# Chunk-selected attention with a squared-ReLU feed-forward: the last sequence's scores on row halves, its mask spread by DMA

## The chip, the cores and the metric

The kernel runs on one core of a Trainium2 chip. Its time is device microseconds of one execution; several executions are given by their median and range. The engines are called PE (TensorE, matrix products; PEld is its weight loads), DVE (VectorE), ACT (ScalarE), POOL (GpSimd) and SP (SyncE, which here only issues DMAs). Each works through its own instructions in order, and so does each queue of DMAs.

## The reference, cut to what matters

Four sequences of 768 positions, eight heads of 64. Keys are cut into 24 chunks of 32. For each query and head an upper bound of its product with any key of a chunk is formed from the chunk's elementwise minimum and maximum; the six chunks with the largest bound (among those not in the future) are kept, and plain causal softmax attention runs over the kept chunks. All of it then goes through a feed-forward layer with a squared ReLU.

```
k_min, k_max = min and max of k over each chunk
ub = sum(maximum(q * k_min, q * k_max), axis=-1)       # one number per query and chunk
ub = where(causal, ub, -1e9)
top_chunks = argsort(ub)[..., -6:]
scores = q @ k.T / sqrt(64)
scores = where(chosen chunk and not in the future, scores, -1e9)
attn = softmax(scores) @ v
x = attn as [3072, 512]
out = maximum(x @ w_in, 0) ** 2 @ w_out                # w_in 512x2048, w_out 2048x512
```

## The kernel before, in words

**Tiles.** A sequence has six tiles of 128 positions. The first tile can choose among at most four chunks, so it needs no selection; the first tiles of all four sequences are treated together at the start (`first_transposes`, `first_attention`, L553 to L605), with their own feed-forward. The other five tiles of each sequence follow, by pairs of heads: sixteen pairs, p = 0 to 15, four for each sequence.

**Stage A of a pair** (`stage_a`, L622) prepares keys and queries with the head dimension on partitions (for sequences 0 and 1 PE turns them, for 2 and 3 the DMA does, `turn_by_dma`, L388), takes chunk minima and maxima on DVE (L697), forms the bounds on PE (L660, L662), finds the sixth largest by MAX8 on DVE (L668) and writes the selection `selb` (L727: 1 where a chunk is not chosen). The selection is turned (by PE, or for sequences 2 and 3 by an SP DMA transpose) and copied under the 64 rows of the queries, into rows 64 to 87 of `qsc`; rows 64 to 87 of `kqc` hold -32768 in the columns of the respective chunk (`kq_rows`, L336). A product over 88 rows is then the score, pushed far down where the chunk isn't chosen. Each pair needs two key copies, two query copies and four selection copies for this, on DVE or ACT (helper `copy`, L281 and L283). Four sets of `kqc` and `qsc` rotate.

**Stage B of a pair** (`stage_b`, L766) has, for each head, five banks of 512 score columns (table `BANKS`): two matmuls of 88 rows (L782), the exponential on ACT (L804), a causal product on DVE or select on POOL for the 128x128 diagonal blocks (`causal`, L756), and four value matmuls with 65 columns (L793; the 65th is the sum of the weights). DVE divides (`normalise`, L609) and writes `x`.

**Feed-forward** (`ffn`, L823): `x` is turned (by DMA for sequences 1 to 3), `up` multiplies by w_in (L866), takes the ReLU (ACT L873, or DVE L875) and the square on DVE (L884), `down` multiplies by w_out (L897), copies the result out of PSUM and stores it with an SP DMA (L910). For the last sequence, `up` uses the score banks.

**What sets the order.** Every operation is given to a planner (class `Plan`, L81) with its engine or engines, a cost, a due time, what it needs and the buffers that it uses. The planner walks through a modelled time: among the operations that could start first on an engine it takes the one due first, and it writes out each engine's list. Buffers of a kind are counted in `Plan({...})` (L266). The due times come from numbers in `P` (L240): a lead for each pair's stage A, a due time and rate for each feed-forward, and so on. Early in the kernel, where the modelled PE waits, it puts in filler products of a constant tile (`keep_warm`, L529) to keep PE active. Loads go through POOL's queue in a fixed order.

The feed-forward work of a sequence is laid among the attention work of the next one; that of the last sequence has nothing beside it.

## Time and profile before

| what | us |
|---|---|
| median of 3 runs | 265.79 |
| lowest, highest | 264.72, 266.02 |
| span of the profiled execution, first to last instruction | 263.6 |
| PE busy in it | 251.4 |
| ACT busy in it | 197.8 |
| DVE busy in it | 183.0 |
| POOL busy in it | 106.4 |

The profiled execution has its span alone as a time of its own; it lies 2.2 us below the median of the runs, which also hold what comes before the first and after the last instruction. In the views below, a row of a group ends with its busy time, the mean of one instruction in nanoseconds, and the time that the engine sat idle just before such an instruction, with what ended that wait. Rows of the chain and of the timeline begin with start and duration in us. Matmuls overlap in their latency: what a stream of them costs is read from the distance of their starts.

### The profile page before, as it was taken

The numbers are of one execution on the slowest core, as the hardware profiler recorded it, in microseconds if no ns is written. First come the engines' busy times: TensorE is split into PE (matmuls) and PEld (weight loads), VectorE is DVE, ScalarE is ACT, GpSimd is POOL, SyncE is SP. The second block draws the span as 40 slices with busy tenths as digits, with TensorE's granted clock in tenths as the row PEclk, the third lists the DMA queues.
The fourth block names the chain that finished last, engine by engine and source line by source line (L and its number), as shares of the span: only waits on it lengthen the run. The fifth ranks groups of instructions, "written<-read, shape, count | busy, mean of one in ns | idle before, by whom it ended". The sixth has DMA issues, their size and how long they took to land.

```text
span 263.6 us, 6555 instructions
## 1 busy us (share of the span) xinstructions
PE 251.4 (95%) x2382; PEld 164.1 (62%) x2405; DVE 183.0 (69%) x663; ACT 197.8 (75%) x395; POOL 106.4 (40%) x185
## 2 busy tenths in 40 slices
PE   6899999999999999999999999998999999999995
PEld 1577566666687666665686645666865564765443
DVE  7569999778999999998999943644757142455000
ACT  6658897859899999999989845987866692677111
POOL 7998987799555599833311201110200010000000
PEclk9799999999999999999999999999999999999999
DMA  8999999999999999995440001154000113400122
GB/s 153 156 175 180 181 198 190 94 126 174 170 151 166 149 157 143 123 145 148 87 93 15 2 20 75 44 82 101 2 0 15 42 44 99 120 2 0 40 82 80
DMA packets 106336, 26.51 MB, mean 101 GB/s; under 512 B 99008, under 2 KB 103360, under 8 KB 106304
## 3 DMA queue, kind: packets, MB, share of 16 engines
q0 software_dynamic: 75088, 13.11, 67.9%
q1 hardware_dynamic: 31216, 12.98, 24.0%
q8 instruction: 19, 0.31, 0.5%
q14 instruction: 13, 0.11, 0.2%
HBM read 27.26 MB, written 6.29 MB: 127 GB/s over the span
## 4 chain that ended last, share of the span: by engine, by line
PE 62%; DVE 24%; ACT 8%; issue 3%; DMA 2%; SPq 0%; ACTq 0%; DVEq 0%
PE py L897 25%; PE ph L866 20%; PE ps L782 8%; PE av L793 4%; DVE h L884 4%; DVE kr L697 4%; DVE m L668 3%; DVE qsc L283 3%; ACT e L804 2%; DMA xT<-x 2%; ACT ht L873 2%; DVE x L614 2%; ACT qsc L281 2%; DVE kqc L283 1%; DVE ubm L722 1%
## 5 line engine op out<-in xcount | busy, mean ns | idle before, releaser
L866 PE MATMUL ph<-xT,w_in_sb 128*128 128x256 bf16 (+2 forms) x592 | 95.7, 304 | 1.6 <-DMA xT<-x 1.2
L804 ACT ACTIVATE e<-ps 128x512 bf16<-128x512 f32 x160 | 86.4, 608 | 7.5 <-PE ps L782 4.4
L897 PE MATMUL py<-w_out_sb,h 128*128 128x512 bf16 (+2 forms) x377 | 87.9, 370 | 1.2
L762 POOL TENSOR_SCALAR_AFFINE_SELECT e<-e 128x128 bf16<-128x128 bf16 (+1 forms) x88 | 31.0, 365 | 101.0 <-ACT e L804 89.1
L866 PEld LDWEIGHTS <-w_in_sb 128*128 128x128 bf16 x592 | 55.6, 97 | 24.9 <-DMA xT<-x 1.6
L873 ACT ACTIVATE ht<-ph 128x384 bf16<-128x384 f32 (+2 forms) x130 | 58.9, 457 | 16.2 <-PE ph L866 12.5
L884 DVE TENSOR_TENSOR h<-ht 128x256 bf16<-128x256 bf16 (+2 forms) x148 | 47.8, 333 | 16.4 <-ACT ht L873 12.9
L897 PEld LDWEIGHTS <-h 128*128 128x128 bf16 x400 | 36.2, 97 | 33.8
L782 PE MATMUL ps<-qsc,kqc 88*128 88x128 bf16 (+1 forms) x320 | 51.7, 272 | 0.3 <-DVE ubm L722 0.2
L782 PEld LDWEIGHTS <-kqc 88*128 88x128 bf16 x320 | 27.6, 97 | 14.8 <-issue 0.8
L281 ACT COPY ob<-py 128x512 f32<-128x512 f32 (+2 forms) x22 | 12.5, 570 | 29.2 <-PE py L897 29.1
L793 PEld LDWEIGHTS <-e 128*128 128x128 bf16 x640 | 29.6, 97 | 6.4 <-issue 0.3
L793 PE MATMUL av<-vn,e 128*128 128x65 bf16 x480 | 29.6, 193 | 0.0
L759 DVE TENSOR_TENSOR e<-e,tri 128x128 bf16<-128x128 bf16 (+1 forms) x40 | 9.7, 242 | 14.9 <-ACT e L804 14.2
L614 DVE TENSOR_TENSOR x<-av,rc 128x320 bf16<-128x320 f32 (+1 forms) x40 | 18.7, 472 | 0.5
L668 DVE MAX8 m<-ubm 128x8 f32<-128x24 f32 x160 | 15.5, 167 | 0.0
L697 DVE TENSOR_REDUCE kr<-kT 128x24 bf16<-128x768 bf16 x16 | 14.8, 951 | 0.2
L697 DVE TENSOR_REDUCE kr<-kt 128x24 bf16<-128x768 bf16 x16 | 14.8, 935 | 0.0
L793 PE MATMUL av<-v,e 128*128 128x65 bf16 x160 | 13.9, 193 | 0.1
L875 DVE TENSOR_SCALAR ht<-ph 128x256 bf16<-128x256 f32 (+2 forms) x18 | 8.2, 454 | 8.2 <-PE ph L866 8.2
L612 DVE RECIPROCAL rc<-av 128x5 f32<-128x5 f32 (+1 forms) x40 | 7.2, 184 | 9.4 <-PE av L793 8.5
L281 ACT COPY qsc<-sT 24x256 bf16<-24x256 bf16 (+1 forms) x29 | 12.4, 427 | 1.6 <-DMA sT<-selb 0.9
(92 smaller groups left out, 258.7 us busy)
## 6 DMA issues: line engine op xcount, KB each, us to landing
out_dram<-ob SPq DMA_DIRECT2D x23, 256.0 KB, 2.2
w_in_sb<-in_moe_w_in_dram POOLq DMA_DIRECT2D x4, 512.0 KB, 7.2
w_out_sb<-in_moe_w_out_dram POOLq DMA_DIRECT2D x4, 512.0 KB, 8.8
vn<-in_v_dram POOLq DMA_DIRECT2D x15, 128.0 KB, 6.9
nt<-in_k_dram POOLq DMA_DIRECT2D x10, 128.0 KB, 6.6
nt<-in_q_dram POOLq DMA_DIRECT2D x10, 128.0 KB, 5.3
kn<-in_k_dram POOLq DMA_DIRECT2D x8, 80.0 KB, 7.0
qn<-in_q_dram POOLq DMA_DIRECT2D x8, 80.0 KB, 5.7
```

Source lines behind the costliest of these rows:

```text
L281: nc.scalar.copy(dst, src)
L614: return plan.op({"DVE": 0.06 + 0.00108 * D * n}, due, lambda _: nc.vector.tensor_mul(x(), av[:, :, 0:D], rc[:, 0:n].unsqueeze(2).to_broad ...
L668: nc.vector.max(out=m8[:, i, hh], in_=ubm[:, i, hh])
L697: nc.vector.tensor_reduce(kr[:, mm].rearrange("d (t c) -> d t c", c=128 // CH) if b >= BY_DMA else kr[:, mm], part(kT).rearrange("d t (c j ...
L762: nc.gpsimd.affine_select(out=e, in_=e, compare_op=ALU.is_ge, fill=0.0, base=0, channel_multiplier=-1, pattern=[[0, n], [1, 128]])
L782: nc.tensor.matmul(ps[:, 128 * c:128 * (c + nt)], lhsT=kqs[:, s, hh, 128 * j:128 * (j + 1)], rhs=qss[:, s, hh, 128 * (t0 - 1):128 * (t0 - ...
L793: nc.tensor.matmul(av[:, t - 1], lhsT=e[:, 128 * c:128 * (c + 1)], rhs=value_tile(b, h, j), start=(i == 0 and c == 0), stop=(i == len(BANK ...
L804: nc.scalar.activation(e.tile, ps.tile, ACT.Exp, scale=scale), [sc], [ps, e])
L866: nc.tensor.matmul(ph.tile, lhsT=w_in_sb[:, ki, 128 * f:128 * (f + 1)], rhs=xT[:, c0 // 128:c1 // 128, ki], start=(ki == 0), stop=(ki == N ...
L873: nc.scalar.activation(ht.tile, ph.tile, ACT.Relu)
L884: {"DVE": 0.067 + w / 1920}, at[0] + P["h2"], lambda _: nc.vector.tensor_mul(h2[f][:, c0:c1], ht.tile, ht.tile), [op], [ht, h2[f]])))
L897: nc.tensor.matmul(py.tile, lhsT=h2[f][:, 128 * t:128 * (t + 1)], rhs=w_out_sb[:, f, c0:c1], start=(f == 0), stop=(f == NFI - 1))
```

## The change

For the last sequence alone (`MASKED = 3`), scores and mask part ways:

- The scores are products over the 64 rows of the head dimension, straight from the turned keys and queries. A pair's two heads lie on partitions 0 to 63 and 64 to 127, and `score_banks` issues them alternately, 128 columns each, so that one head uses one half of PE's rows and the other head the other. Two banks of each head are one operation of 16 matmuls; there are ten such operations.
- The selection (now 1 where a chunk is chosen) is multiplied by 3e38, turned by the SP DMA as before, stored to a DRAM buffer `seen`, and read back by four SP DMAs, each of which repeats every chunk's row over 32 partitions. What lands in `mask` (128 x 21 x 2 x 128) has 3e38 where the key's chunk is chosen by the query, and 0 elsewhere. POOL makes it causal at the five diagonal places.
- After the exponential, DVE takes the minimum of weights and mask (`choose`), for whole banks.
- The extra rows and the copies of keys, queries and selections are no longer made for this sequence.

To make room, two buffers that hold `kqc` and `qsc` for two sets each, the keys and queries of sequence 1 and the masks share three slots (`set`); `kq` falls from 6 to 4 buffers, `e` rises from 6 to 8. The ten output stores of sequences 1 and 2 go from SP's queue to POOL's (`out=(1, 2)`). The planner knows a cost of 0.095 for a switch between 64-row and full matmuls, and its layout is refitted: 249 shifts of due times over ranges of operations (`moves`), a new order of the loads (`order`), another tie width (`wait`).

The diff, cut to its core (the tables of shifts, renamed helpers and moved code left out):

```diff
     BUSY = 0.11
     WARM = 8.0
+    SWITCH = 0.095
...
+                if op.rows != rows:
+                    cost += self.SWITCH
+                rows = op.rows
...
-    P = dict(lead=[0, 207.45, 109.14, 153.29, -29.2, 112.12, 38.49, 53.35, 112.23, 30.95,
+    P = dict(moves=[], order=[], out=(1, 2), lead=[0, 207.45, 109.14, 153.29, -29.2, 112.12, 38.49, 53.35, 112.23, 30.95,
...
+    P.update(moves=[(702, 770, 14.04), (644, 759, -9.08), (940, 964, 20.66), (410,
+             423, 4.85), (679, 756, -9.73), (498, 570, 5.54), (535, 639, 3.35),
...
+             order=[0, 5, 3, 1, 2, 4, 6, 7, 10, 9, 19, 12, 11, 8, 13, 14, 15, 16,
...
+             wait=0.00328)
...
-    plan = Plan({"tp": 1, "ps": 3, "av": 2, "ff": 2, "e": 6, "h2": NFI + 6, "ht": 3,
-                 "ob": 3, "kq": 6, "nt": 6,
+    plan = Plan({"tp": 1, "ps": 3, "av": 2, "ff": 2, "e": 8, "h2": NFI + 6, "ht": 3,
+                 "ob": 3, "kq": 4, "nt": 6, "set": 3, "seen": 3,
...
-    kqs = consts.tile([KC, NSET, 2, S], BF16, tag="kqs", name="kqc")
-    qss = consts.tile([KC, NSET, 2, QC], BF16, tag="qss", name="qsc")
+    sets = [buffer("set", [128, 2, 2, S + QC], name="kqc") for _ in range(2)]
+
+    def kqs(rows, s, *cols):
+        return sets[s // 2][(rows, s % 2, *cols, slice(0, S))]
+
+    def qss(rows, s, *cols):
+        return sets[s // 2][(rows, s % 2, *cols, slice(S, S + QC))]
...
+        both = buffer("set", [128, 2, NS, H, D], name="kqn")
         for nm in "kq":
-            if b < BY_DMA:
+            if b == BY_DMA - 1:
+                nat[nm, b] = both
...
+    def stage_a_turned(p):
+        b, hp = divmod(p, NP)
+        s = p % NSET
+        t0 = HALVES * p - P["lead"][p]
+        op = plan.op
+        kT, qT = turned["k", b], turned["q", b]
+        qp, qm = buffer("qp", [128, QC]), buffer("qm", [128, QC])
+        ub = buffer("tp", [128, NS, 2, NC], F32, name="ub")
+        sT = buffer("st", [128, 2, 128], name="sT")
+        seen = buffer("seen", [2 * 128, 128], name="seen")
+        mask = masks[p] = buffer("set", [128, NM, 2, 128], name="mask")
+
+        def like(t):
+            return t.rearrange("d (t u j) -> d u t j", u=2, j=64)
+
+        kb = chunk_bounds(
+            p, t0, list(loaded["k", b]), kT, lambda t: t[:, :, hp],
+            lambda t: t.rearrange("d t (c j) -> d t c j", j=CH),
+            lambda t: t.rearrange("d (t c) -> d t c", c=128 // CH))
+        sq = halves(qp, qm, lambda: qT[:, :, hp].rearrange("d t (u j) -> d u t j", u=2),
+                    like, list(loaded["q", b]), qT, t0, 0.34)
+        ubm, m8, m = ranked(p, t0, sq, kb, qp, qm, ub)
+        chosen = selbs[:, s].rearrange("p t h c -> p (t h c)")[:, 0:2 * 128]
+
+        def select(i0, i1):
+            n = 4 * (i1 + 1)
+            c0 = 8 * PLACE[i0 + 1, 0]
+            nc.vector.tensor_tensor(
+                chosen[:, c0:c0 + 2 * n * (i1 - i0)].rearrange(
+                    "p (i c h) -> p i h c", h=2, c=n), ubm[:, i0:i1, :, 0:n],
+                m8[:, i0:i1, :, TOPK - 1:TOPK].to_broadcast([128, i1 - i0, 2, n]),
+                op=ALU.is_ge)
+
+        def pick(*runs):
+            for r in runs:
+                select(*r)
+
+        def enlarge():
+            nc.vector.tensor_single_scalar(chosen[:, 0:8 * NM], chosen[:, 0:8 * NM], BIG,
+                                           op=ALU.mult)
+
+        sel = [op({"DVE": 0.23}, t0 + 19, lambda _: pick((0, 2), (2, 3)),
+                  m[:1] + prepared.get((p - NSET, "sT"), []), [ubm, m8])]
+        sel = [op({"DVE": 0.37}, t0 + 19, lambda _: (pick((3, 4), (4, 5)), enlarge()),
+                  m + sel, [ubm, m8])]
+        t = turn_by_dma(lambda: sT.tile, lambda: chosen, t0 + 21, sel, [sT],
+                        640, -0.8)
+        prepared[p, "sT"] = [t]
+        w = op({"SP": 0.45}, t0 + 23, lambda _: nc.sync.dma_start(
+            out=seen.tile.rearrange("(x r) j -> r x j", r=128), in_=sT.tile),
+            [t] + written[-1:], [sT, seen, mask], packets=300, turns=True, late=1.0)
+        written.append(w)
+
+        def spread_rows(g):
+            rows = seen[0:8 * NM].rearrange("(u g h) j -> g u (h j)", g=4, h=2)
+            nc.sync.dma_start(
+                out=mask[32 * g:32 * g + 32].rearrange("c u h j -> c u (h j)"),
+                in_=rows[g].unsqueeze(0).to_broadcast([32, NM, 2 * 128]))
+
+        spread = [op({"SP": 0.50}, t0 + 25 + g, lambda _, g=g: spread_rows(g),
+                     [w], [seen, mask], packets=1850, turns=True, free=True, late=0.2)
+                  for g in range(4)]
+        for i in range(NB):
+            u = [PLACE[x] for x in UNITS[4 * i:4 * i + 4] if x[0] == x[1]][0]
+            prepared[p, "mask", i] = [op(
+                {"POOL": 0.37}, t0 + 30 + i, lambda _, u=u: causal("POOL", mask[:, u], 2),
+                spread, [mask])]
...
+    def score_banks(todo, due):
+
+        def go(_):
+            for p, i in todo:
+                b, hp = divmod(p, NP)
+                kT, qT = turned["k", b], turned["q", b]
+                for c, (t, j) in enumerate(UNITS[4 * i:4 * i + 4]):
+                    for hh in range(2):
+                        rows = slice(D * hh, D * hh + D)
+                        nc.tensor.matmul(bank(p, hh, i)[:, 128 * c:128 * (c + 1)],
+                                         lhsT=kT[rows, j, hp], rhs=qT[rows, t - 1, hp],
+                                         start=True, stop=True)
+
+        for n, (p, i) in enumerate(todo):
+            for hh in range(2):
+                bursts[p, hh, i] = buffer("tp" if n and hh else "ps", [128, 512], F32,
+                                          name="ps")
+        seqs = sorted({p // NP for p, _ in todo})
+        sc = plan.op({"PE": 0.225 * len(todo)}, due, go,
+                     [o for b in seqs for nm in "kq" for o in loaded[nm, b]]
+                     + scored_last[-1:],
+                     [bank(p, hh, i) for p, i in todo for hh in range(2)]
+                     + [turned[nm, b] for b in seqs for nm in "kq"], rows=64)
+        scored_last.append(sc)
+        for n, (p, i) in enumerate(todo):
+            for hh in range(2):
+                stage_b_turned(p, hh, i, sc, due + 4 * n + 2 * hh)
...
+    def stage_b_turned(p, hh, i, sc, due):
+        b, hp = divmod(p, NP)
+        h = 2 * hp + hh
+        ps = bank(p, hh, i)
+        e = buffer("e", [128, 512])
+        if i == 0:
+            sums[p, hh] = buffer("av", [128, NS, D + 1], F32), None
+        av, prev = sums[p, hh]
+
+        def values(_):
+            for c, (t, j) in enumerate(UNITS[4 * i:4 * i + 4]):
+                nc.tensor.matmul(av[:, t - 1], lhsT=e[:, 128 * c:128 * (c + 1)],
+                                 rhs=value_tile(b, h, j),
+                                 start=(i == 0 and c == 0), stop=(i == NB - 1),
+                                 skip_group_check=True)
+
+        done = plan.op({"ACT": 0.48}, due + 0.5, lambda _: nc.scalar.activation(
+            e.tile, ps.tile, ACT.Exp, scale=scale), [sc], [ps, e])
+        u = PLACE[UNITS[4 * i]]
+        def choose(_):
+            seen = masks[p][:, u:u + (4 if i else 6), hh]
+            like = e.tile.rearrange("p (u j) -> p u j", j=128)
+            if not i:
+                seen = seen.rearrange("p (a b) j -> p a b j", b=3)[:, :, 0:2]
+                like = like.rearrange("p (a b) j -> p a b j", b=2)
+            nc.vector.tensor_tensor(like, like, seen, op=ALU.min)
+
+        done = plan.op({"DVE": 0.39}, due + P["vm"], choose,
+            [done] + prepared[p, "mask", i], [e, masks[p]])
+        prev = plan.op({"PE": 0.125}, due + P["va"], values,
+                       [done, prev, made["ones", b]] + loads_of("v", b, hp),
+                       [e, av, nat["v", b]])
+        sums[p, hh] = av, prev
+        if i == NB - 1:
+            x = inputs[b]
+            x_done[b, 1].append(normalise(
+                av, NS, lambda: x[:, :, D * h:D * (h + 1)], prev, [x], due + 7))
...
-            plan.op({"SP": 0.35}, at[0] + 1, lambda _: nc.sync.dma_start(
-                out[rows[t]:rows[t] + 128, c0:c1], ob.tile), [op], [ob],
-                packets=2 * w, turns=True)
+            plan.op({"POOL": 0.80} if by_pool else {"SP": 0.35}, at[0] + 1, lambda e: (
+                nc.gpsimd if e == "POOL" else nc.sync).dma_start(
+                    out[rows[t]:rows[t] + 128, c0:c1], ob.tile), [op], [ob],
+                packets=2 * w, turns=not by_pool, free=by_pool)
...
+            if b < MASKED:
+                stage_a(p)
+                stage_b(p, x)
+            else:
+                stage_a_turned(p)
+        if b == MASKED - 1:
+            for c in range(MASKED, B):
+                x_done[c, 1] = []
+        if b >= MASKED:
+            todo = [(p, i) for p in range(NP * b, NP * (b + 1)) for i in range(NB)]
+            for n in range(0, len(todo), 2):
+                score_banks(todo[n:n + 2], HALVES * NP * b + 4 * n)
...
+    for i0, i1, change in P["moves"]:
+        for op in computed[i0:i1]:
+            op.due += change
+    if P["order"]:
+        plan.loads = [plan.loads[i] for i in P["order"]]
```

More of the change, by code (lines that the diff above doesn't have):

```diff
@@ L40, in __init__ @@
         self.fill = 0
+        self.rows = 128
 class Transfers:
@@ L102, in op @@
     def op(self, where, due, fn, needs=(), tiles=(), packets=0, turns=False,
-           late=0.0):
+           late=0.0, rows=128, free=False):
         op = Op(where, due, fn, [n for n in needs if n is not None],
@@ L108, in op @@
         op.late = late
-        op.number = -1 if packets and not turns else len(self.ops) - len(self.loads)
+        op.rows = rows
+        op.load = bool(packets) and not turns and not free
+        op.number = -1 if op.load else len(self.ops) - len(self.loads)
         self.ops.append(op)
-        if packets and not turns:
+        if op.load:
             self.loads.append(op)
@@ L126, in order @@
         ready = [op for op in self.ops if not count[op]]
-        landed, done = [], []
+        landed, done, loads = [], [], 0
+        rows = 128
         dma = Transfers()
@@ L131, in order @@
             for op in ready:
-                if op.packets and not op.turns and op is not self.loads[len(landed)]:
+                if op.load and op is not self.loads[loads]:
                     continue
@@ L386, with natural @@
                                        name=nm + "t")
+    def natural(nm, b):
+        t = nat[nm, b].tile
+        return t[:, "kq".index(nm)] if b == BY_DMA - 1 and nm in "kq" else t
     def turn_by_dma(dst, src, due, needs, tiles, packets=1270, late=0.0):
@@ new lines @@
+    NM = NU + 1
+    NB = NU // 4
+    PLACE = {(t, j): j + (0, 0, 3, 6, 10, 15)[t] for t, j in UNITS}
+    masks = {}
+    written = []
+    def stage_a_turned(p):
+        b, hp = divmod(p, NP)
+        s = p % NSET
+        t0 = HALVES * p - P["lead"][p]
[54 more added lines that the diff above has]
+                spread, [mask])]
@@ L820, in stage_b, with bank @@
                 prev, [x], due + 7))
-    def ffn(x, ready, rows, by_dma, due, rate, up_tags=("ff", "ff")):
+    bursts = {}
+    def bank(p, hh, i):
+        return bursts[p, hh, i]
+    def score_banks(todo, due):
[21 more added lines that the diff above has]
+        for n, (p, i) in enumerate(todo):
+            for hh in range(2):
+                stage_b_turned(p, hh, i, sc, due + 4 * n + 2 * hh)
@@ L825, in ffn @@
+    def ffn(x, ready, rows, by_dma, due, rate, up_tags=("ff", "ff"), by_pool=False):
         n = len(rows)
```

101 lines of the change are left out of this document (76 added, 25 removed), and 72 rows, old and new, of tables (order, sel).

## Prediction

> **What bounds the kernel now.** I read the page's first two parts, then the stretches, then the chain that ended last, then the idle time of TensorE.
>
> ```profile
> span 263.6 us, 6555 instructions
> PE 251.4 (95%) x2382; PEld 164.1 (62%) x2405; DVE 183.0 (69%) x663; ACT 197.8 (75%) x395; POOL 106.4 (40%) x185
> PEclk9799999999999999999999999999999999999999
> PE py L897 25%; PE ph L866 20%; PE ps L782 8%; PE av L793 4%; DVE h L884 4%; DVE kr L697 4%; DVE m L668 3%; DVE qsc L283 3%; ACT e L804 2%; DMA xT<-x 2%; ACT ht L873 2%; DVE x L614 2%; ACT qsc L281 2%; DVE kqc L283 1%; DVE ubm L722 1%
> ```
>
> TensorE (PE) is busy for 95% of the span at full clock, and its four big products head the chain. The stretches, from the view that sums busy time by window (the columns are PE, PEld, DVE, ACT, POOL, clock, DMA):
>
> ```profile
> 0.00:25.00 25.00, 20.36 (x210) 13.97 (x211) 17.54 (x61) 16.75 (x28) 22.45 (x35) 0.93 1.70 164
> 100.00:150.00 50.00, 49.33 (x530) 33.61 (x535) 47.87 (x197) 46.82 (x97) 20.29 (x45) 1.00 0.86 98
> 150.00:226.00 76.00, 74.36 (x666) 46.48 (x674) 36.80 (x138) 51.35 (x104) 4.95 (x15) 1.00 0.20 51
> ```
>
> The reader is to see two things. Only the first 25 us leave PE idle for long (4.6 us, and part of its busy time there is filler, below). And 150 to 226 us, where the last sequence's attention runs beside the feed-forward work of the sequence before, is PE's alone: VectorE (DVE) is busy for 48% of it, ScalarE (ACT) for 68%, GpSimd (POOL) for 7%, the DMA for little. Before that stretch, at 100 to 150, DVE and ACT are nearly full. So a change that takes PE work out of the late stretch and gives DVE and DMA work there trades scarce for plentiful, if nothing that it adds comes late.
>
> **The change part by part.**
>
> *Scores of the last sequence.* Before, a bank of 512 scores of one head takes two or three matmuls over 88 rows; the chain has three banks in a row, and the page's group has all of them. The one place where the kernel already runs two heads on row halves is the first-tile attention, in the timeline:
>
> ```profile
> 206.13 0.66 PE ps L782 x6
> 14.23 0.22 PE xt L286 x4
> 15.08 0.40 PE L286 MATMUL xt<-ident,x 128*128 128x128 bf16 x4
> 15.41 0.40 PE L583 MATMUL ps<-t,t 64*128 64x128 bf16 x8
> 15.41 0.23 PE L583 MATMUL ps<-t,t 64*128 64x128 bf16 x2
> 15.59 0.22 PE L583 MATMUL ps<-t,t 64*128 64x128 bf16 x1
> 15.74 0.28 PE L539 MATMUL ph<-warm 128*128 128x256 bf16 x1
> ```
>
> Three banks in 0.66 us are 0.22 us a bank; the last sequence has 4 pairs x 2 heads x 5 banks = 40, so 8.8 us. At 15.41 two of the 64-row matmuls start together (the row with x2), and the last of eight starts at 15.59: four pairs in three steps of 0.06 us, so the halves do run side by side. The change issues 4 x 20 = 80 such pairs: 80 x 0.058 = 4.6 us. But each group of pairs stands between full-height matmuls. Around 15.4 the four transposes before end their issue by about 15.31 (four from 15.08 at 0.055, as in the chain's row at 14.23) and the pair starts at 15.41: 0.10 us lost; behind, 15.59 + 0.06 to 15.74: 0.09 us. The changed program has 10 such groups, none next to another, so 20 switches x 0.095 = 1.9 us. Sum: 4.6 + 1.9 - 8.8 = **-2.3 us**, on PE, in a stretch where PE is the bound. Bounds: nothing for a switch if those two gaps were waits for data (-4.2 us); a whole 0.22 us matmul latency each (4.4 us: the gain is gone, +0.2).
>
> The Trainium skill speaks against this part: "TensorEngine Tiling (Array Packing)", section Tiling Modes, Key Properties, says that changing the tiling mode drains the engine. The two gaps of 0.10 and 0.09 us agree with it, and no other row here tests it; without the rule the sum would be the -4.2 us of the first bound.
>
> *The mask.* Before, the selection went into 24 extra rows of queries and keys, by copies on DVE and ACT; these 8 key copies, 8 query copies and 16 selection copies go, and with them 32 causal selects. In come, for each of 4 head pairs, a scaling of the selection, a transpose by DMA (it was there), a store of it to DRAM, four DMAs of 344 KB that spread it over 32 partitions each, five causal selects on POOL, and ten minimum operations of 128x512 on DVE. Rows for these:
>
> ```profile
> L884 DVE TENSOR_TENSOR h<-ht 128x512 bf16<-128x512 bf16 x12 | 5.1, 429 | 0.0
> L762 POOL TENSOR_SCALAR_AFFINE_SELECT e<-e 128x256 bf16<-128x256 bf16 x20 | 8.6, 431 | 12.2 <-ACT e L804 10.1 <-issue 1.9
> L281 ACT COPY kqc<-kt 64x768 bf16<-64x768 bf16 x9 | 7.4, 827 | 0.1
> out_dram<-ob SPq DMA_DIRECT2D x23, 256.0 KB, 2.2
> out_dram<-ob SPq DMA_DIRECT2D x1, 64.0 KB, 1.6
> sT<-selb SPq DMA_TRANSPOSE x8, 2.3
> L283 DVE COPY qsc<-sT 24x384 bf16<-24x384 bf16 (+1 forms) x35 | 10.0, 285 | 1.3 <-PE sT L286 0.5
> L389 SPq DMA_TRANSPOSE xT<-x x15: 1194/1264/2842, 123.7 to 225.4; - x15
> 162.47 2.27 ACT L804 ACTIVATE e<-ps 128x512 bf16<-128x512 f32 x4 [0.30 <-PE av L793]
> ```
>
> DVE: 40 x 0.43 = 17.2 us more, less its share of the copies (its count of them falls by 23, about 0.3 us each, 7 us) and of the causal products (10 fewer, 2.5 us): some +8 us. ACT loses copies worth about 7 us. With 37 of 76 us busy before, DVE has room; cost nothing. If the minimum ran at twice this duration, DVE would stand at 37 + 25 = 62 of 76 us, and would begin to hold PE by its order. POOL: 20 x 0.43 = 8.6 us in place of the selects that it loses; nothing.
>
> The chain behind one mask: transpose 2.3, store 1.6 (the 64 KB row), four spreads, five selects. Stores of 64 and 256 KB differ by 0.6 us, so 344 KB take 1.1 us of queue; four take 4.4 and land 1.4 later. 2.3 + 1.6 + 5.8 + 2.2 = 12 us. The order shows what covers it. The scores no longer wait for the selection, only the minimum does, and eight banks of exponentials may wait (buffers e 6 -> 8). The masks of the first two pairs are issued before or while the third sequence's attention ends; those of the last two stand on SP behind the five transposes of its result, and are wanted when PE has done about 19 and 25 us of work more. Behind 5 x 1.3 us of transpose issue and two masks (2 x 6 us) that is 18.5 and, with the selects, 21: cover of a few us. I take nothing; this is the part with the thin cover, priced below.
>
> *Where the attention ends.* After the last group of pairs the order holds 4.1 us of other PE work before the last 28 value matmuls, and 48 matmuls of 512 columns (10.4 us) after them, before the last feed-forward needs the transposed result; before it was 6.85 us:
>
> ```profile
> 218.85 6.85 PE py L897 x31
> 225.71 1.31 PE ph L866 x12
> 174.51 0.88 SPq L389
> 175.44 5.17 DMA xT<-x
> 180.65 0.61 PE ph L866 x4
> PE ph L866 <- DMA xT<-x: 1.2, 1, 1.2
> ```
>
> The first is enough for four exponentials (2.3 us, the row at 162.47) and a minimum (0.4 us), some 3 us with hand-overs, and the second for transposes of 5.2 us. The one wait of PE on such a transpose, 1.2 us up to 180.65, stands where the third sequence's result turns. There the new order has 5.9 us of PE matmuls and four switches (0.4) between the last value product and the first user, against 0.9 of issue, 5.2 of transfer and some 0.7 us of normalising: 0.5 us is left. **-0.7 us**; bounds -1.2 and, if two masks' spreads run in front of those transposes in the queue, +2.
>
> *Start and refit.* Due times of hundreds of operations and the order of the loads change, so the first 25 us are laid out anew. The planner puts filler matmuls where it leaves PE waiting for over 0.3 us; they are rows of the trace:
>
> ```profile
> L539 PE MATMUL ph<-warm x28: 272/273/284, 15.7 to 23.1; 128*128 128x256 bf16 x28
> L286 PE MATMUL qT<-ident,warm x8: 217/219/220, 20.1 to 20.5; 128*128 128x128 bf16 x8
> 15.80 1.64 PE ph L539 x14
> ```
>
> 28 x 0.117 + 8 x 0.055 = 3.7 us; the changed program has 6 and 16: 1.6 us. PE is thus laid out to wait 2.1 us less. Not all of it need come true, since what it waits for is data; I take half, **-1.0 us**, with -2.1 and +1 as ends. What moves between engines there is in it.
>
> *Stores by POOL.*
>
> ```profile
> L447 POOL DMA_DIRECT2D vn<-in_v_dram x15 | 13.4, 924 | 0.0
> L910 SPq DMA_DIRECT2D out_dram<-ob x25: 332/333/531, 54.2 to 260.8; - x25
> ```
>
> Ten stores of the second and third sequence go from SP to POOL, 0.9 us of POOL each instead of 0.33 of SP, in a stretch where POOL was busy for 5 of 76 us; the last stores stay on SP. Nothing.
>
> **Sum.** -2.3 - 0.7 - 1.0 = -4.0 us, against the profiled execution's span of 263.6, so 259.6. The runs shown have a median of 265.79; the 2.2 us around the span stay as they are: **261.8 us**.
>
> **The rivals.**
>
> 1. *Masks late (slower).* Each spread reads the same rows 32 times in 512-byte pieces, and no row of this trace does that. If a spread holds the queue for 2.2 us, the whole of a 256 KB store with nothing overlapped, the last two masks slip by 8 x 1.1 = 8.8 us, less some 2 us of cover; the minimum then blocks DVE's queue, the squares stand behind it, and PE waits 6.8 us: 265.8 - 4.0 + 6.8 = 268.6 us. It decides from 8 x (t - 1.1) - 2 = 4.0, t = 1.85 us. For it: DRAM reads of this kind are unseen. Against it: the DMA is nearly idle there (its column reads 0.20, against 1.70 in the first 25 us).
> 2. *The pairs bring nothing.* Switches at a full latency, and the refit gives nothing at the start: +0.2 - 0.7, 265.3 us. For it: one place in the trace has the switch. Against it: both of its gaps are under half a latency.
> 3. *The change doesn't do what it says.* If the two heads ran one after the other, 160 x 0.055 = 8.8 us and 1.9 for switches: +1.9 in place of -2.3, so +0.2 in all, 266.0 us. The x2 row at 15.41 speaks against it.
> 4. *The refit pays in full.* -2.1 at the start, -1.2, the switches hidden (-4.2): 258.3 us.
>
> **How the numbers follow.** Forecast 0.60, rival 1 0.18, rivals 2 and 3 together 0.10, rival 4 0.12. The range reaches from just under rival 4 to under rival 1's price, where part of its cases (a slip of 4 to 5 us) still lies: 257.5 to 267.0 us; it leaves out rival 1's upper part. 0.5% is 1.3 us, about what a measurement of this kernel can tell from no change: faster is the forecast and rival 4 (0.72), within it rivals 2 and 3 (0.10), slower rival 1 (0.18).
>
> **What would show it.** Right: 64-row matmuls in pairs at 0.06 us, gaps of 0.1 us at their edges; spreads that land 2 to 2.5 us after issue; in the late stretch no PE wait on DVE's minimum; less idle time and filler before 25 us than the 4.6 and 3.7 us of before. Wrong: a wait of PE's value matmuls on the minimum, and of that on a mask; PE waiting on the third sequence's transposes for over 1.2 us; DVE over 80% busy from 150 us on; a slower start.

## The result, and the profile after

The changed kernel takes 262.16 us (median of four runs, 261.07 to 262.89), beside 265.41 us (264.72 to 266.02) of the kernel before on the same chip: 3.3 us less. The ratio is 0.9852 with a 95% interval of 0.9812 to 0.9891; ratios, here and below, are estimated from the runs that a slower state of the chip did not disturb, and lie up to 0.003 beside the quotient of the medians. The gain is clear of noise, and it is under 2%. The forecast was 4.0 us less and 261.8 us. The profiled execution spans 261.2 us against 263.6; a second profile of the same kernel, below, spans 260.2.

The first lines of its page, its clock row, and the chain that ended last, by line:

```profile
span 261.2 us, 6709 instructions
PE 249.4 (95%) x2471; PEld 160.3 (61%) x2471; DVE 191.0 (73%) x692; ACT 188.6 (72%) x379; POOL 115.2 (44%) x194
PEclk9599999999999999999999999999999999999999
PE py L1199 28%; PE ph L1168 25%; PE ps L1008 7%; PE av L1020 4%; ACT e L1032 4%; DMA v<-in_v_dram 4%; ACT kqc L368 4%; PE ps L1065 2%; DVE kqc L370 2%; PE av L1098 2%; DVE h L1186 2%; DVE kr L845 1%; DVE m L816 1%; DVE ht L1177 1%; POOL k L462 1%
```

PE is still the bound, at 95%. DVE has 8.0 us more than before and ACT 9.2 us less. The stretches, in the windows of the prediction:

```profile
0.00:25.00 25.00, 18.93 (x182) 12.38 (x183) 15.34 (x57) 15.06 (x25) 20.52 (x33) 0.86 1.59 154
150.00:226.00 76.00, 75.98 (x785) 47.01 (x784) 47.18 (x154) 49.36 (x103) 16.13 (x33) 1.00 0.58 118
```

From 150 to 226 us PE now shows no gap at all (75.98 of 76, 74.36 before). DVE rose by 10.4 us in that stretch and POOL by 11. The stretch ahead of it, 100 to 150 us, is nearly as it was (PE 49.7 us, 49.3 before). The first 25 us went the other way: PE is busy for 18.9 us instead of 20.4, and the clock reads 0.86 instead of 0.93. What PE waited for in the whole execution, the longest first:

```profile
PE T L373 <- DVE q L370: 2.0, 2, 1.2
PE av L692 <- DMA v<-in_v_dram: 1.4, 1, 1.4
PE wt L641 <- DVE behind L421: 1.1, 1, 1.1
```

All three lie in the first 25 us. Between 150 and 226 us the list of PE's waits is empty, where before it held the 1.2 us for the third sequence's transposes. (The rest of the difference there is mostly a matter of records: in the trace before, 23 of the 400 products with w_out have no record, though their weight loads have; they are counted in below.) So the sum can be read in three parts: work that PE no longer does, waits in the middle, and the start.

To size them I added up the issue time of every matmul by its shape, as steady streams of that shape show it (0.216 us for 512 columns, 0.162 for 384, 0.110 for 256, 0.055 for 128, 0.031 for 65, some 0.02 for 48, and half of it for a 64-row product that runs beside another), and took what is left of each stretch as time lost, fillers included.

| us | before | after | the same kernel again |
|---|---|---|---|
| PE's useful work in all | 238.1 | 233.9 | 233.9 |
| lost in the first 25 us | 14.8 | 15.5 | 15.0 |
| lost from 25 to 226 us | 7.2 | 8.5 | 8.0 |
| of these, switches to and from row halves | | 1.9 | 1.9 |

Useful work falls by 4.2 us, as the sum had it (8.8 - 4.6). The switches give back 1.9. The other losses between 25 and 226 us fall by 0.6 and by 1.1 us (-0.7 was forecast). The start loses 0.7 and 0.1 us more, where 1.0 less was forecast. That makes -2.2 and -3.3 us; the two spans differ from 263.6 by -2.4 and -3.4, and the rest lies behind 226 us.

The pairs themselves, in the timeline of PE:

```profile
169.44 0.28 PE L1020 MATMUL av<-vn,e 128*128 128x65 bf16 x4
169.66 0.62 PE L1065 MATMUL ps<-qt,kt 64*128 64x128 bf16 x16
170.21 0.30 PE L1020 MATMUL av<-vn,e 128*128 128x65 bf16 x4
```

From the start of the sixteen 64-row products to the start of what follows are 0.55 us: eight pairs at 0.057 make 0.46, and the switch back 0.09. In front, four value products of 0.031 end their issue at 169.57, and the pairs start at 169.66: 0.09 us for the switch there. All ten groups show the same two gaps, 0.092 to 0.096 us in and 0.092 out.

The mask, by its tile (the issues of the spreads on SP in ns, then the time from issue to landing in us), and the minimum's group in the page:

```profile
L956 SPq DMA_DIRECT2D mask<-seen x16: 303/544/3696, 143.6 to 193.5; - x16
DMA to landing us min/median/max: 4.4/7.8/11.3
```

```profile
L1112 DVE TENSOR_TENSOR e<-e,mask 128x512 bf16<-128x512 bf16 x40 | 17.4, 457 | 3.2 <-ACT e L1103 2.2
```

The minimum is as dear as thought (0.457 us, 17.4 in all, against 0.43 and 17.2). The spreads are not: 7.8 us from issue to landing instead of 2 to 2.5. How long one holds the queue is read from the selects behind the last two masks, in the timelines of POOL and DVE:

```profile
195.84 2.41 POOL L988 TENSOR_SCALAR_AFFINE_SELECT mask<-mask 128x256 bf16<-128x256 bf16 x5 [12.54 <-DVE x L716]
203.06 2.21 POOL L988 TENSOR_SCALAR_AFFINE_SELECT mask<-mask 128x256 bf16<-128x256 bf16 x5 [4.82 <-DMA mask<-seen]
```

```profile
196.36 0.60 DVE L1112 TENSOR_TENSOR e<-e,mask 128x512 bf16<-128x512 bf16 x1 [0.30 <-POOL mask L988]
203.51 1.14 DVE L1112 TENSOR_TENSOR e<-e,mask 128x512 bf16<-128x512 bf16 x2 [0.30 <-POOL mask L988]
```

The last mask lands 7.2 us behind the one before it, four spreads: 1.8 us each, not 1.1. (The first row's wait is put down to DVE, but line 716 writes nothing that POOL's select reads; what it waited for are the spreads.) DVE starts its minimum 0.5 us behind the start of POOL's first select, both times after waiting for it. The few us of cover are used up as far as DVE goes, and the list of PE's waits still holds none for it. But PE has next to nothing left either, as two rows at the last mask show:

```profile
204.79 0.49 DVE L716 TENSOR_TENSOR x<-av,rc 128x320 bf16<-128x320 f32 x1
205.34 0.20 PE L1098 MATMUL av<-v,e 128*128 128x65 bf16 x1
```

The division on DVE stands behind the first two minima with this mask, and frees the sums (`av`) that PE's next value product writes: it ends at 205.28 us, 0.06 us ahead of that product. The repeat profile shows the same 0.06 us.

How late the masks are for the prediction's sum can be read from SP:

```profile
171.29 7.66 SPq L490 DMA_TRANSPOSE xT<-x  x5
```

Counted from there, the third mask's last spread lands after 24.4 us and the fourth's after 31.7; the sum had 12.5 (6.5 + 6) and 18.5. The first value products with these masks start after 29.2 and 34.0 us, where the prediction, if it counted from the same moment, had about 19 and 25.

### The profile page after: what moved, and what is told of

Its sections match the earlier page's. It is cut to its first block, busy times and chain, and to the rows that moved or that the text cites. A ratio compares the mean times of both kernels' runs of the same rounds, so it can differ in the third digit from the quotient of the medians.

```text
span 261.2 us, 6709 instructions
## 1 busy us (share of the span) xinstructions
PE 249.4 (95%) x2471; PEld 160.3 (61%) x2471; DVE 191.0 (73%) x692; ACT 188.6 (72%) x379; POOL 115.2 (44%) x194
## 4 chain that ended last, share of the span: by engine, by line
PE 70%; DVE 11%; ACT 9%; DMA 4%; POOL 3%; issue 2%; ACTq 0%; POOLq 0%
PE py L1199 28%; PE ph L1168 25%; PE ps L1008 7%; PE av L1020 4%; ACT e L1032 4%; DMA v<-in_v_dram 4%; ACT kqc L368 4%; PE ps L1065 2%; DVE kqc L370 2%; PE av L1098 2%; DVE h L1186 2%; DVE kr L845 1%; DVE m L816 1%; DVE ht L1177 1%; POOL k L462 1%
## 5 line engine op out<-in xcount | busy, mean ns | idle before, releaser
L1175 ACT ACTIVATE ht<-ph 128x384 bf16<-128x384 f32 (+2 forms) x120 | 53.3, 451 | 18.7 <-PE ph L1168 14.0
L1186 DVE TENSOR_TENSOR h<-ht 128x256 bf16<-128x256 bf16 (+2 forms) x148 | 47.6, 332 | 10.6 <-ACT ht L1175 8.2
L988 POOL TENSOR_SCALAR_AFFINE_SELECT e<-e 128x128 bf16<-128x128 bf16 (+1 forms) x66 | 24.4, 377 | 43.8 <-ACT e L1032 42.8
L1008 PE MATMUL ps<-kqc 88*128 88x128 bf16 (+1 forms) x240 | 39.4, 272 | 0.7 <-ACT e L1032 0.6
L368 ACT COPY ob<-py 128x512 f32<-128x512 f32 (+2 forms) x24 | 13.8, 575 | 29.2 <-PE py L1199 29.2
L1008 PEld LDWEIGHTS <-kqc 88*128 88x128 bf16 x240 | 19.8, 97 | 11.3 <-issue 1.1
L1020 PEld LDWEIGHTS <-e 128*128 128x128 bf16 x480 | 21.6, 97 | 4.5 <-POOL e L988 0.5
L1177 DVE TENSOR_SCALAR ht<-ph 128x256 bf16<-128x256 f32 (+2 forms) x28 | 13.7, 492 | 11.7 <-PE ph L1168 11.5
L1020 PE MATMUL av<-vn,e 128*128 128x65 bf16 x360 | 21.7, 193 | 0.0
L1112 DVE TENSOR_TENSOR e<-e,mask 128x512 bf16<-128x512 bf16 x40 | 17.4, 457 | 3.2 <-ACT e L1103 2.2
L988 POOL TENSOR_SCALAR_AFFINE_SELECT mask<-mask 128x256 bf16<-128x256 bf16 x20 | 9.2, 496 | 20.9 <-DVE x L716 12.5
L845 DVE TENSOR_REDUCE kr<-kT 128x24 bf16<-128x768 bf16 x16 | 14.8, 953 | 0.9 <-PE kT L373 0.8
L368 ACT COPY kqc<-sT 24x384 bf16<-24x384 bf16 (+1 forms) x27 | 11.7, 434 | 4.3 <-PE sT L373 2.6
```

What stands on the lines that cost most here:

```text
L368: nc.scalar.copy(dst, src)
L845: nc.vector.tensor_reduce(kr[:, mm].rearrange("d (t c) -> d t c", c=128 // CH) if b >= BY_DMA else kr[:, mm], part(kT).rearrange("d t (c j ...
L988: nc.gpsimd.affine_select(out=e, in_=e, compare_op=ALU.is_ge, fill=0.0, base=0, channel_multiplier=-1, pattern=[[0, n], [1, 128]])
L1008: nc.tensor.matmul(ps[:, 128 * c:128 * (c + nt)], lhsT=kqs(slice(0, KC), s, hh)[:, 128 * j:128 * (j + 1)], rhs=qss(slice(0, KC), s, hh)[:, ...
L1020: nc.tensor.matmul(av[:, t - 1], lhsT=e[:, 128 * c:128 * (c + 1)], rhs=value_tile(b, h, j), start=(i == 0 and c == 0), stop=(i == len(BANK ...
L1175: nc.scalar.activation(ht.tile, ph.tile, ACT.Relu)
```

## The experiments

All times are medians, and each ratio is to the kernel before on the same chip. Against it the changed kernel stands at -3.3 us.

**The same kernel again**, as the yardstick for the others.

> The changed kernel unaltered, as the mark for its companions on this chip. Theory (the gain is TensorE work saved in the last sequence's scores, net of the switches): 0.985 of the time before, 261.5 to 262.5 us. Rival (a good part of the 3 to 4 us is chance of the start, since the profiled spans differ by 2.4 us only): 0.990 or more.

262.44 us (261.95 to 264.43), ratio 0.9856 (0.9796 to 0.9917), -3.3 us again. Runs of one kernel spread over 2 us and more, and the intervals reach up to 1.7 us to each side with four runs and 0.9 with ten, so differences below about 1.5 us between two experiments are not told apart.

### The pairs of row halves

**More switches.** Between the two units of each group stands a full-height matmul of one column:

```
-            for p, i in todo:
+            for n, (p, i) in enumerate(todo):
...
+                if n:
+                    nc.tensor.matmul(bank(p, 0, i)[:, 0:1], lhsT=warm, rhs=warm[:, 0:1],
+                                     start=True, stop=True)
```

> Between the two units of each of the ten score groups stands one full-height matmul of one column, overwritten by the next product. Theory (each change between 64-row and full-height matmuls costs 0.095 us in each direction): ten groups x 0.19 us, about 2 us slower than the changed kernel, and 20 gaps of 0.095 more in the trace. Rival (the gaps at the edges of a group are waits for data or for the weights): 0.3 us slower at most.

264.5 us, ratio 0.994 (0.9906 to 0.9974): -1.3 us, 2.1 more than the unaltered kernel beside it. In PE's timeline:

```profile
169.31 0.40 PE L1068 MATMUL ps<-qt,kt 64*128 64x128 bf16 x8
169.63 0.18 PE L1063 MATMUL ps<-warm 128*128 128x1 bf16 x1
169.74 0.40 PE L1068 MATMUL ps<-qt,kt 64*128 64x128 bf16 x8
170.07 0.30 PE L1020 MATMUL av<-vn,e 128*128 128x65 bf16 x4
```

Four pairs (0.23 us) and a gap of 0.09 to the one column, 0.11 from there to the next pairs: 0.2 us more in each of the ten groups, 2.0 us in all, which the time shows in full. A switch costs what the gaps say, and PE's queue is where the time is decided.

**Both heads on one half.** The second head's scores are left out and the first head's made twice, so that every product lies on rows 0 to 63:

```
-                        rows = slice(D * hh, D * hh + D)
+                        rows = slice(0, D)
```

> Both heads' products of a pair use rows 0 to 63 (so the second head's scores are left out and the first head's made twice); nothing can overlap. Theory (the pairs side by side save 0.056 us each against one after the other): 80 x 0.056 = 4.5 us slower than the changed kernel, the gain gone. Rival (TensorE's work there is not what sets the time): under 2 us slower.

266.51 us, ratio 1.0029 (0.9999 to 1.006): +0.9 us, 4.2 us over the changed kernel.

```profile
168.12 1.06 PE L1065 MATMUL ps<-qt,kt 64*128 64x128 bf16 x16
169.12 0.30 PE L1020 MATMUL av<-vn,e 128*128 128x65 bf16 x4
```

1.00 us to the next operation instead of 0.55, ten times: 4.5 us. This is the third rival's case made real (it gave 266.0): without the overlap of the halves the whole change is worth nothing.

**Heads in turn.** Within each unit four products of one head come first, then four of the other:

```
-                for c, (t, j) in enumerate(UNITS[4 * i:4 * i + 4]):
-                    for hh in range(2):
+                for hh in range(2):
+                    for c, (t, j) in enumerate(UNITS[4 * i:4 * i + 4]):
```

> In each group the four products of one head come first, then the four of the other, in place of taking turns. Theory (two heads overlap only when their matmuls are neighbours on different row halves): 16 x 0.055 = 0.89 us a group in place of 0.45, so some 4 us slower than the changed kernel, back at the time before. Rival 1 (the halves run ahead of one another however they are ordered): no change. Rival 2 (most of the gain is not from the pairs): slower by under 2 us.

261.62 us, ratio 0.9824 (0.9768 to 0.9879). My theory, that neighbours must alternate to overlap, fell: the group takes 0.57 us instead of 0.55.

```profile
168.65 0.64 PE L1065 MATMUL ps<-qt,kt 64*128 64x128 bf16 x16
169.22 0.30 PE L1020 MATMUL av<-vn,e 128*128 128x65 bf16 x4
```

**Eight and eight.** The same over both units, eight of one head and then eight of the other:

> All eight products of one head of a group first, then the eight of the other. With four and four there was no loss: 16 matmuls still started within 0.42 us. Theory A (each half works through its own matmuls, some way ahead of the other): no change. Theory B (the look-ahead is about four matmuls with their weights): about half of the overlap goes, 2 us slower than the changed kernel.

264.1 us, ratio 0.9955 (0.992 to 0.999): 1.8 us over the changed kernel.

```profile
169.08 0.86 PE L1065 MATMUL ps<-qt,kt 64*128 64x128 bf16 x16
169.87 0.30 PE L1020 MATMUL av<-vn,e 128*128 128x65 bf16 x4
```

0.79 us, about midway between 0.55 and 1.00. The starts in the trace show why: of the first head's eight, four start alone at 0.00, 0.07, 0.12 and 0.18 us; from 0.23 to 0.42 both halves start products side by side; the second head's last four are alone again. In both orders a product starts up to about four places ahead of its turn if its half is free, so PE does not keep strictly to the order of its list, as the opening has it of every engine. Four and four loses next to nothing, and eight and eight half of the gain.

### The mask

**No minimum.** `choose` returns at once, so that attention runs unmasked in the last sequence and DVE has 40 operations less; spreads and selects stay.

> The minimum of weights and mask is left out for the last sequence (40 VectorE operations; masks are still made, nothing reads them), all else in the same order. Theory (TensorE waits neither for the minimum nor for the mask): within 0.5 us of the changed kernel. Rival (masks late, or VectorE too full): 1 us or more faster.

261.76 us, ratio 0.9827 (0.9764 to 0.989), 0.7 us from the unaltered kernel and within its spread. The late stretch:

```profile
150.00:226.00 76.00, 75.73 (x787) 47.21 (x785) 32.65 (x113) 49.07 (x104) 14.23 (x32) 1.00 0.59 118
```

DVE has 14.5 us less to do there, and PE does the same. In the changed kernel neither the minimum nor the mask's lateness costs anything that can be told.

**Each minimum twice.** 40 more DVE operations of the same kind, nothing else:

```
             nc.vector.tensor_tensor(like, like, seen, op=ALU.min)
+            nc.vector.tensor_tensor(like, like, seen, op=ALU.min)
```

> Each minimum is done twice over, 40 more VectorE operations of about 0.4 us. The prediction's text has VectorE at 62 of 76 us then, with TensorE beginning to wait for it. Theory (VectorE has room): under 1.5 us slower than the changed kernel. Rival (VectorE's place in the order is the cover): 3 us or more slower.

271.7 us, ratio 1.0244 (1.021 to 1.0279): 9.4 us over the changed kernel. Windows and waits of PE in the late stretch:

```profile
150.00:226.00 76.00, 67.26 (x715) 41.56 (x723) 60.51 (x186) 46.26 (x95) 13.27 (x30) 1.00 0.51 101
```

```profile
PE av L1098 <- DVE e L1113: 4.5, 4, 2.0
PE ph L1169 <- DVE ht L1178: 2.5, 3, 1.1
PE av L1098 <- DVE x L716: 0.9, 1, 0.9
```

17 us more of DVE make 9.4 us, with DVE busy for 80% of the stretch. The first minimum fits beside PE's work without cost, a second does not. Value matmuls wait for the minimum, and the feed-forward's products for DVE's ReLUs (`ht`), which are queued behind it and free the PSUM bank that the product needs.

**Every spread twice**, the second of each pair to a buffer that nobody reads:

```
+    spare = dpool.tile([128, 21, 2 * 128], BF16, tag="spare", name="spare")
...
                 in_=rows[g].unsqueeze(0).to_broadcast([32, NM, 2 * 128]))
+            nc.sync.dma_start(
+                out=spare[32 * g:32 * g + 32],
+                in_=rows[g].unsqueeze(0).to_broadcast([32, NM, 2 * 128]))
```

> After each spread of a mask a second DMA of the same size and the same source goes to unused DRAM, so the queue time of a mask doubles. In the changed kernel a spread takes about 1.8 us of queue, and the minimum starts within 0.1 us of its mask, while TensorE doesn't wait. Theory (the cover is used up): the masks of the last two pairs come 7 and 14 us later, and TensorE waits for at least 5 us. Rival (buffers and other work still cover some us): under 2 us slower.

287.53 us, ratio 1.0806 (1.0745 to 1.0866): +21.3 us, 24.6 over the changed kernel. The waits of PE:

```profile
PE av L1102 <- DVE x L716: 7.0, 1, 7.0
PE ps L1012 <- ACT kqc L368: 5.7, 1, 5.7
PE ph L1172 <- DMA xT<-x: 4.7, 1, 4.7
```

That is too coarse to size the cover, so the next one adds less.

**One spread more for each mask**, four in all, behind the first (`if g == 0:` in front of the added call, and a `spare` of 32 rows).

> One extra transfer of a spread's size behind the first spread of each mask, to unused DRAM: four in all, 1.8 us of queue each. Sixteen cost 25 us. Theory (no cover is left): 4 us or more slower than the changed kernel. Rival (there is cover of 2 to 4 us for each mask, which the sixteen ran through): within 1 us.

266.5 us, ratio 1.0047 (1.0014 to 1.0081): 4.2 us over the changed kernel. The four transfers do not lengthen the masks alike. From the first spread's landing to the last's, the first mask takes 9.7 us (5.8 and 6.4 in the two profiles of the changed kernel), the second 6.4 (5.5 and 6.0), and the last two together 15.8 (15.1 and 13.1). The two longest waits of PE from 120 to 226 us, and the chain where the first of them ends:

```profile
PE ps L1012 <- ACT kqc L368: 2.3, 1, 2.3
PE av L1102 <- DVE x L716: 1.1, 1, 1.1
```

```profile
149.13 8.66 DMA sT<-selb
157.81 0.52 ACT kqc L368
158.37 1.01 PE ps L1012 x4
```

The first wait isn't at a mask. SP's queue holds the first mask's spreads in front of the third sequence's last selection, and that transpose lands 8.7 us after its issue; its scores are what PE waits for (in the changed kernel it lands after 4.7 and 5.6 us). From 158.3 to 161.7 us, from the end of this wait on, the granted clock reads 0.50, which makes the wait dearer than its 2.3 us. The second wait is at the last mask, on the division that had 0.06 us to spare: DVE stands 1.4 us for that mask. Who pays for a longer spread is whoever stands behind it in the queue.

### The refit, the start, the stores

**Without the refitted times.** The list of moved due times, the order of the loads and the changed wait are taken out (`P.update(...)` removed); pairs, mask and stores stay.

> The change without its refit: no shifts of due times, the order of the loads and the tie width of before. Theory (the refit carries what hides the mask chain): the scores still save 2.3 us of TensorE work, but masks and transposes come late; 2 to 8 us slower than the changed kernel, with TensorE waiting in the late stretch. Rival (the refit does little beside the pairs): within 1 us of the changed kernel.

273.5 us, ratio 1.0288 (1.0236 to 1.0339): 7.3 us slower than before, 10.6 over the changed kernel. The chain behind the last sequence's attention:

```profile
221.96 2.63 DVE e L1036 x6
224.63 1.10 ACT e L1027 x2
...
228.02 1.20 SPq L414
229.26 2.54 DMA xT<-x
231.94 19.29 PE ph L1092 x128
```

The last minimums and values stand directly in front of the transposes (issued at 228.0 us), and PE has nothing left to do beside them: its longest wait, 4.9 us, is for `xT`. The products behind that wait start at half the clock, so the same 128 take 19.29 us where the changed kernel needs 17.39. The stretches behind the wait, 17 products in the first and 34 in the second:

```profile
232.00:235.50 3.50, 3.50 (x17) 2.39 (x18) 0.88 (x3) 1.15 (x3) 0.00 (x0) 0.50 0.67 91
235.50:239.00 3.50, 3.50 (x34) 3.13 (x32) 2.05 (x7) 3.00 (x8) 0.00 (x0) 0.99 0.09 18
```

The changed kernel has this instead:

```profile
213.00 10.36 PE py L1199 x48
223.37 17.39 PE ph L1168 x128
```

The 48 products of 10.4 us that the prediction named as cover stand there, and the last feed-forward follows without a gap. The change in operations and the new order belong together; the first alone loses.

**The first loads in their old order**, since the waits of the start name a load of values: the first six POOL loads as before, the rest as in the changed kernel.

> The first six loads of POOL in the order of before (q, k, v, v, q, k), all else as laid out. Theory (the start lost 0.7 us because value tiles land later, a wait of 1.4 us for one at 18.5 us): TensorE has lost 14.5 to 15 us by 25 us in place of 15.5, and the time falls by 0.5 to 1 us. Rival (the start is slower for the clock, two windows at half in place of one): no change.

264.53 us, ratio 0.992 (0.9885 to 0.9954): 1.6 us slower than the changed kernel by the medians, at the edge of what can be told, and not faster. The theory fell. PE's first wait is then another one:

```profile
PE T L373 <- DMA k<-in_k_dram: 2.7, 1, 2.7
```

The wait of 1.4 us for the values is gone, and one of 2.7 us for keys is there. The new order of PE's work wants those keys earlier.

**All stores by SP** (`out=()` in place of `out=(1, 2)`).

> The ten stores of the second and third sequence by SP again, refit kept. Theory (SP's queue is what the masks and transposes share, and a store that waits there for its copy holds them up): 0 to 1.5 us slower than the changed kernel, with later masks. Rival (where the stores are issued is worth nothing): within 0.5 us.

261.52 us, ratio 0.9835 (0.978 to 0.9889): -4.7 us, and the interval overlaps that of the changed kernel, so no worth of the ten stores that POOL took over is shown either way. One of the five runs, the profiled one, took 264.2 us, the others 261.35 to 261.7; in it PE waits 1.9 us for the third sequence's transposes.

## Why the prediction came out as it did

It was right in direction and near in size: 3.3 us less for 4.0 forecast. Step by step:

- **Scores, -2.3.** Right to a tenth of a microsecond. Useful work fell by 4.2 us and 20 switches of 0.09 us took 1.9 back. That both halves run at once is shown by the kernel that puts both heads on one (4.2 us dearer), and the switch by ten more excursions (2.1 us dearer). The Trainium skill's rule in "TensorEngine Tiling (Array Packing)", section Tiling Modes, Key Properties, that a change of tiling mode drains the engine, agrees with the gaps of 0.09 us in all ten groups; without it the sum would have forecast 1.9 us too much. The second rival (a full latency per switch) is out.
- **DVE, nothing.** Right: +8.0 us over the whole, and leaving the minimum out brings nothing that can be told. The warning beside it was right as well: with the minimum twice, DVE stands at 60.5 us of the window (62 was named), and it holds PE.
- **Mask, nothing, with thin cover.** The outcome was right, but in good part by luck: two sizes were wrong and cancelled. A spread holds the queue for 1.8 us, not 1.1, and lands after 7.8 us, and the last mask is there 31.7 us behind the first of the transposes instead of 18.5. PE wants it only after 34.0 us, where the prediction had about 25. By the first rival's own formula a spread of 1.8 us would have cost 3.6 us (8 x 0.7 - 2), and nothing of the kind is seen; at 1.85 it put the point where the gain is gone. With 0.06 us left at the last mask the case lay on the line and not, as a chance of 0.18 suggests, well inside it. The 344 KB (336 in the page's count) were priced by bytes, from 256 KB stores, and "land 1.4 later" by a store's tail. What a row of the trace could not show was the price of a transfer that repeats a row over 32 partitions in pieces of 512 bytes: in the trace the median packet of it takes 44 to 49 ns on its DMA engine, and a 512-byte packet of a store 26 ns; 672 packets of 46 ns on 16 engines are 1.9 us. Reading one row 32 times is not all of it: with every spread doubled, half of the packets read the same rows in the same pieces but go to DRAM, and about four in five of all of them take 30 ns or less. The rival's path appears at the last mask, with 1.1 us of waiting for four transfers more and 7.0 for sixteen. It was wrong in part: the first wait to appear is that of the third sequence's scores for their selection, behind the first masks in SP's queue, and at the last mask it is the division that PE waits for, not the squares. What 2.25 us for each spread would cost is not measured, since the four transfers fell mostly on the first mask.
- **Third sequence's transposes, -0.7.** Right: the whole wait of 1.2 us is gone, not 0.7 of it, and no other took its place (0.6 and 1.1 us less lost by the two profiles).
- **Where the attention ends, nothing.** Right; the chain runs through the 48 products into the last feed-forward.
- **Start, -1.0.** Wrong: by 25 us PE has lost 15.0 to 15.5 us, and 14.8 before. The fillers became fewer as read (28 and 8 before, 6 and 16 after, some 2 us less), but PE's idle time there grew from 4.6 us to 6.1 and 5.9, and what is lost in all did not fall. The step that failed is reading fewer fillers as less idle time. The planner lays out fillers where it foresees a wait; some waits of the start come from loads it placed otherwise. Two rows of the start, in the timeline of PE:

```profile
17.49 1.05 PE L1168 MATMUL ph<-xT,w_in_sb 128*128 128x256 bf16 x8 [0.49 <-DMA w_in_sb<-in_moe_w_in_dram]
19.94 0.40 PE L692 MATMUL av<-v,e 128*128 128x65 bf16 x8 [1.41 <-DMA v<-in_v_dram]
```

PE stands 1.9 us for two loads that did not hold it before (in the repeat for the second alone). They are not the whole of it, since moving the first six loads back only exchanged the wait. The clock in that window was also lower (0.86 against 0.93), but it does not order the losses: of the experiments that leave the start alone, the doubled spreads read 0.86 there and lose 14.4 us, and eight and eight reads 1.00 and loses 15.2. All nine of them lie between 14.4 and 15.4 us, about the one profile of before, so neither a gain nor a loss of the start is shown. Which part of the new layout keeps the start from gaining stays open.

- **Stores, nothing.** Right, as far as can be told.

The refit was priced only through the start. What else it does was in the prediction as cover, read from the new order; the kernel with the old times shows what such covers are worth. Added up as above, its profile is 10.5 us longer than the changed kernel's: nothing at the start, 3.1 us between 25 and 226 us, and 7.4 behind that, mostly the wait of 4.9 us for the last transposes and the 1.9 us of half clock that follow it.

## What to carry to other kernels

When work moves from the bound engine to idle ones, the idle share says little; what counts is how late the moved work may be and what stands behind it in the same queue. Here DVE at 62% of the stretch, and masks for which it waits 0.3 us, cost nothing that can be told, while 17 us more on the one or a single transfer more for each mask on the other cost 9.4 and 4.2 us. That nothing waits does not say how much room is left: look at how close the next user starts. And a long wait of PE cost more here than its own length, by the half clock behind it. Price a DMA by a row with the same packets, not by its bytes, and count fillers as a planner's forecast, not as a measurement.

## What the runs showed of the hardware

- An excursion of PE from full-height to 64-row products and back costs 0.19 us (0.095 in, 0.092 out), the same in ten of ten groups.
- Products on the two row halves overlap without alternating one by one: four and four is nearly as fast as one and one (0.57 and 0.55 us for sixteen), eight and eight loses half (0.79), all on one half takes 1.00, each counted to the start of the next operation.
- A DMA that repeats 21 pieces of 512 bytes over 32 partitions (336 KB) holds its queue for 1.8 us, some 190 GB/s, and several in a row land 4.4 to 11.3 us after their issue.
- Behind the first 25 us, the granted clock falls to 0.50 towards the end of each of the five waits of PE of 2.3 us or more in these traces (2.3 with one spread more, 4.9 with the old times, 5.7, 4.7 and 7.0 with the spreads doubled). It stays there for 3.4 us at the shortest of them and for 6.8 at the others, most of it in the work behind the wait. At none of the waits up to 2.0 us there does it fall.
- Stores issued by POOL land 0.3 us later than those by SP in the median, as the page of the changed kernel shows:

```profile
out_dram<-ob SPq DMA_DIRECT2D x13, 256.0 KB, 2.6
out_dram<-ob POOLq DMA_DIRECT2D x10, 256.0 KB, 2.9
```
